# Window attention and a gated FFN on one core: the mask of 26 heads moves from VectorE into the score bank on TensorE

## The chip, the cores and the metric

The kernel runs on one core of a Trainium2 chip. The core has a matrix engine (TensorE, PE in the profile), VectorE (DVE), ScalarE (ACT), GpSimd (POOL), a queue engine that starts transfers (SyncE, SP), an on-chip memory (SBUF) and eight accumulation banks (PSUM) into which PE writes. The metric is the device time of one execution in microseconds (us). The kernel before takes 924.29 us, the median of 3 runs that lie between 923.28 and 925.11.

## What is computed

There are two stages. The first is attention with 8 batches, 8 heads, 512 local and 32 global rows and head dimension 64, all in float32. A local row sees the 32 global rows and the local rows at most 32 positions away. The second is an FFN over all 4352 rows, 512 to 2048 to 512 wide, with the gate `h * erf(softplus(h))`.

```
s_g = scale * q_g @ k_all.T;  out_g = softmax(s_g) @ v_all          # 32 global rows see all 544
s_ll = where(|i - j| <= 32, scale * q_l @ k_l.T, -1e9)
s_lg = scale * q_l @ k_g.T
out_l = softmax(concat(s_lg, s_ll)) @ concat(v_g, v_l)
x = concat(out_g, out_l)   as [8 * 544, 512]
h = x @ w_in;  out = (h * erf(softplus(h))) @ w_out
```

## The kernel before

**Attention.** Two heads share one load of queries and keys (`qk`, or `q` and `k` apart) and are scored together: 64 matmuls of 32 query rows against a window of 128 keys fill two PSUM banks `s`, one for each head, with 4 tiles of 128 by 128. For every head `mask_max` (VectorE) then adds a constant mask from SBUF (`mask`, part of the constants `cs`), writes the masked scores `sm` to SBUF and keeps the row extreme in `mx`, one instruction of its own for each of the 4 tiles. For the first 20 heads (`NBIAS`) ScalarE takes the exponentials in 4 instructions with `mx` as their bias; from head 20 on VectorE or GpSimd subtracts `mx` first, and ScalarE takes one exponential over all 512 columns. For the first 28 heads (`TURN`) PE transposes the probabilities back into the score bank `s`, VectorE or ScalarE copies them to `pt`, and 16 more matmuls with the values `va` and `vb` give the output in `s` again; for later heads VectorE transposes in blocks and two transfers through HBM (`tp`, `px`, `pt`) do the rest, with the output in a bank `o`. Every four heads the 32 global rows are done in banks `ga` and `gb`; `GTURN` says for how many of these groups PE makes the transposes.

**FFN.** To keep float32 accuracy every operand is split into a high and a low part (`xh`, `xl`, `winh`, `winl`, `wouth`, `woutl`, `gh`, `gl`), and every product is three matmuls of 512 columns. A batch is one chunk of 512 rows: 8 units `h` of 12 matmuls each, gates of 4 units on ScalarE (with a change of its function table ahead of softplus, of erf and of the next exponential), and 4 row tiles `op` of 24 matmuls. Pass 0 handles one half of the hidden width and pass 1 the other; only 4 of the 8 row blocks of the weights fit at a time. The weights arrive as 64-bit floats (`raw_in`, `raw_out`) and are turned into float32 (`top_in`, `top_out`) by `bits` on VectorE: a multiplication by a power of two, a shift, and two joint bit operations; 16 such pieces are turned during the first 150 us, 16 more near the end of pass 0.

**The order.** The kernel is written as a list of operations with their engines, a key and a guessed duration. `Program.schedule` plays them through on a model of the engines, takes the operation with the smallest key that is ready, chooses between the engines that an operation allows, and so fixes the order of every engine's instructions before the kernel is compiled. On the chip each engine runs its own list strictly in that order and waits where an operand is missing. While the model's PE has nothing to do before the time `FILL`, it puts in matmuls on a constant (`spare`) that keep the clock of PE up. These are real instructions: they take their time whether the data is there or not. So the numbers at the head of the file (keys, leads, `BIAS`, `HARM`, `SLACK`, ...) are priorities; a change of them moves instructions on all engines.

All work of a kind is issued through a helper, so that the profile shows L339 for every matmul, L340 for transposes on PE, L341 for ScalarE, L342 for its table changes, L343 for transfers and L351 for VectorE and GpSimd. The tile names tell them apart.

## Time and profile before

| what | us |
|---|---|
| median of 3 runs | 924.29 |
| the profiled execution's own time | 923.82 |
| its span in the profile | 921.9 |
| PE busy | 901.1 |
| VectorE busy | 639.3 |
| ScalarE busy | 514.3 |
| GpSimd busy | 400.9 |

The profiled execution is one of the kind that was timed: its time is 1.9 us more than its span, the part ahead of the first and behind the last recorded instruction. In the profile "busy" is the time in which at least one instruction of an engine runs. On PE the instructions overlap: a matmul of 512 columns has a duration of 0.39 us, but the next one starts 0.23 us later, so the cost of one in a row is the distance between starts. The same holds on VectorE, to a lesser degree.

### The profile page before, as it was taken

The page shows a single profiled execution, that of the slowest core. Times are in us where ns is not written, and L with a number is a line of the kernel's source. Part 1 is how long each engine was busy: PE and PEld are TensorE (multiplying, and loading weights), DVE is VectorE, ACT ScalarE, POOL GpSimd, SP SyncE. Part 2 cuts the span into 40 slices and gives each one's busy share as a digit, 9 for nine tenths or more (in the row PEclk, how much of TensorE's full clock was granted, in tenths as well). Part 3 has the DMA queues.
Part 4 walks back from the last instruction along what each step waited for, and adds up shares of the span by engine and source line. Part 5 has one row for each costly group of instructions (what it writes and reads, how often), then busy time and mean ns, then how long its engine had stood idle before and what let it go on. Part 6 is the DMA issues. An engine that isn't in the chain of part 4 may idle for free.

```text
span 921.9 us, 23134 instructions
## 1 busy us (share of the span) xinstructions
PE 901.1 (98%) x9363; PEld 751.5 (82%) x9363; DVE 639.3 (69%) x1616; ACT 514.3 (56%) x891; POOL 400.9 (43%) x318
## 2 busy tenths in 40 slices
PE   9889899999999999999999999999999999999998
PEld 7667667777777777878888888899898989999896
DVE  3799998565646766575589897868558575848533
ACT  4557956275645656455576655644646444546461
POOL 0212474164414343243366677735535455534320
PEclk9989999999999999999999999999999999999999
DMA  9788867597886887775462410222222250512203
GB/s 366 256 286 294 252 211 240 183 303 225 291 240 197 303 258 267 253 218 171 143 178 69 161 47 0 46 69 47 77 61 92 46 137 2 137 39 77 69 23 114
DMA packets 89322, 148.66 MB, mean 161 GB/s; under 512 B 11520, under 2 KB 52480, under 8 KB 89216
## 3 DMA queue, kind: packets, MB, share of 16 engines
q1 hardware_dynamic: 89024, 146.93, 50.9%
q8 instruction: 73, 1.20, 0.5%
q10 hardware_dynamic: 192, 0.26, 0.1%
q14 instruction: 33, 0.27, 0.1%
HBM read 108.89 MB, written 38.27 MB: 160 GB/s over the span
## 4 chain that ended last, share of the span: by engine, by line
PE 82%; DVE 12%; POOL 3%; issue 2%; ACT 1%; DMA 0%; DVEq 0%; POOLq 0%; ACTq 0%
PE op L339 37%; PE h L339 33%; PE s L339 4%; DVE top_out L351 3%; PE o L339 2%; PE spare L339 2%; DVE top_in L351 2%; PE ga L339 2%; DVE sm L351 1%; PE go L339 1%; DVE xh L351 1%; DVE xl L351 1%; PE s L340 1%; POOL xl L351 1%; DVE woutl L351 0%
## 5 line engine op out<-in xcount | busy, mean ns | idle before, releaser
L339 PE MATMUL op<-wouth,gh 128*128 128x512 f32 x544 | 217.3, 399 | 0.0
L339 PE MATMUL op<-woutl,gh 128*128 128x512 f32 x544 | 212.9, 391 | 0.0
L339 PE MATMUL op<-wouth,gl 128*128 128x512 f32 x544 | 212.5, 391 | 0.0
L351 POOL TENSOR_TENSOR sp<-sp,hs 128x512 f32<-128x512 f32 x94 | 135.0, 1453 | 165.1 <-ACT sp L341 120.1
L339 PE MATMUL h<-xh,winh 128*128 128x512 f32 (+1 forms) x464 | 165.2, 356 | 0.0
L339 PE MATMUL h<-xl,winh 128*128 128x512 f32 (+1 forms) x464 | 162.2, 350 | 0.2 <-POOL xl L351 0.2
L339 PE MATMUL h<-xh,winl 128*128 128x512 f32 (+1 forms) x464 | 162.2, 349 | 0.0
L351 POOL TENSOR_TENSOR gl<-sp,gh 128x512 fp32r<-128x512 f32 x78 | 111.9, 1442 | 103.9 <-ACT gh L341 72.8
L351 DVE TENSOR_TENSOR hs<-h,hs 128x256 f32<-128x256 f32 x196 | 76.4, 420 | 69.3 <-PE h L339 62.7
L339 PEld LDWEIGHTS op<-wouth,gh 128*128 128x128 f32 x544 | 102.5, 188 | 23.3 <-issue 2.0
L339 PEld LDWEIGHTS op<-wouth,gl 128*128 128x128 f32 x544 | 102.4, 188 | 22.3
L341 ACT ACTIVATE gh<-sp 128x512 fp32r<-128x512 f32 x113 | 69.2, 628 | 90.8 <-PE op L339 27.9
L339 PEld LDWEIGHTS op<-woutl,gh 128*128 128x128 f32 x544 | 102.6, 189 | 18.4
L342 ACT ACT_TABLE_LOAD x90 | 115.5, 1283 | 2.3 <-PEq L1281 0.7
L339 PEld LDWEIGHTS h<-xh,winh 128*128 128x128 f32 x464 | 87.8, 189 | 14.6 <-issue 1.0
L339 PEld LDWEIGHTS h<-xl,winh 128*128 128x128 f32 x464 | 87.9, 189 | 12.5 <-POOL xl L351 0.6
L339 PEld LDWEIGHTS h<-xh,winl 128*128 128x128 f32 x464 | 87.7, 189 | 11.6
L341 ACT ACTIVATE hs<-h 128x512 f32<-128x512 f32 (+1 forms) x66 | 36.5, 553 | 99.0 <-PE h L339 99.0
L341 ACT ACTIVATE sp<-hs 128x512 f32<-128x512 f32 x136 | 76.0, 622 | 16.1 <-DVE hs L351 15.7
L341 ACT ACTIVATE sp<-sp 128x512 f32<-128x512 f32 x136 | 74.8, 620 | 0.4
L351 POOL TENSOR_TENSOR sm<-sm,mx 128x512 f32<-128x512 f32 x26 | 28.7, 1112 | 101.3 <-DVE mx L351 93.7
L351 DVE CUSTOM_DVE_ANT_0 sm<-s,cs 128x128 f32<-128x128 f32 x256 | 57.1, 283 | 22.5 <-PE s L339 20.3
(176 smaller groups left out, 1603.6 us busy)
## 6 DMA issues: line engine op xcount, KB each, us to landing
vb<-in_vB_dram SPq DMA_DIRECT2D x32, 650.0 KB, 6.7
qk<-in_qk_dram SPq DMA_DIRECT2D x30, 656.0 KB, 6.7
rx<-xsc SPq DMA_DIRECT2D x52, 256.0 KB, 5.2
va<-in_vA_dram SPq DMA_DIRECT2D x32, 390.0 KB, 5.2
px<-tp SPq DMA_DIRECT2D x72, 128.0 KB, 4.3
pt<-px SPq DMA_DIRECT2D x18, 512.0 KB, 5.2
raw_in<-in_w_in_dram SPq DMA_DIRECT2D x16, 512.0 KB, 3.9
xsc<-xT SPq DMA_DIRECT2D x32, 256.0 KB, 4.5
```

Of the source, the lines that this page charges most:

```text
L339: pe = lambda n, *a, **k: pinned(nc.tensor.matmul(n, *a, **k))
L340: tr = lambda *a, **k: pinned(nc.tensor.transpose(*a, **k))
L341: act = lambda *a, **k: pinned(nc.scalar.activation(*a, **k))
L342: table = lambda name: pinned(nc.scalar.preload_act_table_set(name))
L351: return lambda *a, **k: pinned(f(*a, **k))
```

## The change

Five things change in the code.

1. For the first 26 heads (`PREMASK`) the mask no longer passes through VectorE's `mask_max`. At the start VectorE makes a bf16 copy of the mask (0 or -2^33) and of a unit matrix (`M16`, once). Ahead of the scores of a pair of heads PE writes the mask into each of the two banks by one bf16 matmul of 512 columns, and the 64 score matmuls add to it. VectorE takes the row maximum of each head by one plain reduction over the bank and multiplies the 4 maxima by -scale. ScalarE takes the exponentials from the bank, in 4 instructions with that bias, so heads 20 to 25 lose the subtraction and gain 3 ScalarE instructions; heads from 26 on subtract as before (`NBIAS` no longer decides).
2. The first step of `bits` (the multiplication by `REBASE`) becomes an operation of its own that ScalarE or VectorE may do.
3. PE transposes probabilities for 26 heads in place of 28, and for 7 groups of global rows in place of 8.
4. `FIRST` goes from 8 to 10: two more heads borrow FFN buffers for their attention tiles.
5. The priorities are new; several of them are now given by pass or by batch.

```diff
-SINCE, COLD, FILL, TICK, HEAT = 0.75, 3.5, 47.058, 3.41, 3200
+SINCE, COLD, FILL, TICK, HEAT = 0.75, 3.5, 52.16, 3.41, 3200
-HKEYS = ((0, -7.476), (4, -4.154), (22, 1.289), (64, 44.267))
+HKEYS = ((0, -7.916), (4, -4.313), (22, 2.061), (64, 45.265))
...
-FIRST = 8
+FIRST = 10
...
-NBIAS = 20
+NBIAS, PREMASK = 19, 26
...
-TURN, GTURN = 28, 8
+TURN, GTURN = 26, 7
...
+    M16 = Buf(mp, [P, 512], F32, "mask16", "os", 2)
...
+    def shorten():
+        m, i = halves()
+        dve.tensor_scalar(m, cs[:, :512], -1.0, -(2.0**33), op0=ALU.is_lt, op1=ALU.mult)
+        dve.tensor_copy(i, ident)
...
+                for n in range(2 if early else 0):
+                    m16, i16 = halves()
+                    pe(SS[n].ap.rearrange("p t k -> p (t k)"), i16, m16, start=True, stop=False)
...
-                                start=True,
-                                stop=True,
+                                start=not early,
+                                stop=not early or t == 3,
...
-        add({"DVE": 0.9}, key, mask_max, [S, CS], [SM, MX])
-        def exps():
+        def exps(src, k):
             for t in range(4):
-                act(SM.ap[:, t, :], SM.ap[:, t, :], AF.Exp, bias=MX.ap[:, t : t + 1], scale=-1.0)
+                act(SM.ap[:, t, :], src[:, t, :], AF.Exp, bias=MX.ap[:, t : t + 1], scale=k)
+        def plain_max():
+            dve.tensor_reduce(MX.ap, S.ap, axis=AX.X, op=ALU.max)
+            dve.tensor_scalar(MX.ap, MX.ap, -scale, None, op0=ALU.mult)
+        if early:
+            add({"DVE": 0.75}, key, plain_max, [S], [MX])
+            add({"ACT": 1.28}, key, lambda: exps(S.ap, scale), [S, MX, TAB], [SM])
+        else:
+            add({"DVE": 0.9}, key, mask_max, [S, CS], [SM, MX])
...
-            dve.tensor_scalar(TOP.ap.bitcast(F32), word(1).bitcast(F32), REBASE, None, op0=ALU.mult)
...
-        add({"DVE": 2.14}, key, bits, [RAW], [TOP])
+        add({"ACT": 0.62, "DVE": 0.42}, key, rebase, [RAW], [TOP])
+        add({"DVE": 1.72}, key, bits, [RAW], [TOP])
```

Three places show how the lists of the engines change. A name such as `s_6_0_2767` is the score bank 0 of the pair that begins with head 6; the last number only counts buffers, and the batch isn't printed. The first place is PE's list at its start, the scores of the first two heads. Before:

```order
L339 LDWEIGHTS const-bfloat16-1.0
L339 MATMUL spare<-const-bfloat16-1.0 128x256
L339 MATMUL s_0_0_188<-qk_0_124 32x128 x4
L339 MATMUL s_0_1_189<-qk_0_124 32x128 x4
...
L339 LDWEIGHTS const-bfloat16-1.0
L339 MATMUL spare<-const-bfloat16-1.0 128x256
```

Now:

```order
L339 LDWEIGHTS const-bfloat16-1.0
L339 MATMUL spare<-const-bfloat16-1.0 128x256
L339 LDWEIGHTS mask_194
L339 MATMUL s_0_0_213<-mask_194 128x512
L339 LDWEIGHTS mask_194
L339 MATMUL s_0_1_214<-mask_194 128x512
L339 MATMUL s_0_0_213<-qk_0_126 32x128 x4
L339 MATMUL s_0_1_214<-qk_0_126 32x128 x4
```

Two mask matmuls stand ahead of the scores. Before, 43 fillers (`spare`) stood ahead of these scores and 171 in all; now 61 stand ahead of them, and 176 in all.

The second place is VectorE's list around the maximum of head 6 of batch 1. Before:

```order
L351 COPY gxT_0_1388<-gb_0_1075 128x64
L351 STREAM_TRANSPOSE xT_3_1390<-xn_2_1241 128x512
L351 TENSOR_SCALAR top_in_3_1_1396<-raw_in_3_1_1085 128x512
L351 TENSOR_SCALAR top_in_3_1_1396<-top_in_3_1_1396 128x512
L351 SCALAR_TENSOR_TENSOR top_in_3_1_1396<-raw_in_3_1_1085,top_in_3_1_1396 128x512 x2
L351 ISA sm_6_1424,mx_6_1425<-s_6_0_1352,cs 128x128
L351 ISA mx_6_1425 128x1
```

Now:

```order
L351 COPY gxT_0_1445<-gb_0_1093 128x64
L351 TENSOR_REDUCE mx_6_1447<-s_6_0_1354 128x4
L351 TENSOR_SCALAR mx_6_1447<-mx_6_1447 128x4
L351 TENSOR_REDUCE mx_7_1452<-s_6_1_1355 128x4
L351 TENSOR_SCALAR mx_7_1452<-mx_7_1452 128x4
L351 TENSOR_SCALAR top_in_2_1_1450<-top_in_2_1_1450 128x512
L351 SCALAR_TENSOR_TENSOR top_in_2_1_1450<-raw_in_2_1_1260,top_in_2_1_1450 128x512 x2
```

The pair of rows `ISA sm` and `ISA mx`, which came four times for a head, has become one reduction and one small product, and the row `top_in<-raw_in` of this piece of the weights is gone from VectorE's list (it is in ScalarE's). Of the 16 pieces of the first 150 us, 10 lose this row.

The third place is PE's list ahead of the first output product of the FFN (`op_0_0`), in batch 3 of the attention. Before:

```order
L339 MATMUL s_4_0_2790<-qk_2_2654 32x128 x4
L339 MATMUL s_4_1_2791<-qk_2_2654 32x128 x4
...
L339 MATMUL ga_0_2621<-va_0_2197,gt_0_2744 32x65 x2
L339 MATMUL ga_0_2621<-va_1_2486,gt_0_2744 32x65 x2
...
L339 MATMUL op_0_0_2863<-wouth_0_1579,gh_0_0_1875 128x512
L339 MATMUL op_0_0_2863<-woutl_0_1580,gh_0_0_1875 128x512
```

Now:

```order
L339 MATMUL s_6_0_2767<-qk_3_2583 32x128 x4
L339 MATMUL s_6_1_2768<-qk_3_2583 32x128 x4
...
L339 MATMUL h_1_5_2845<-xh_1_0_2187,winh_2_688 128x512
L339 MATMUL h_1_5_2845<-xl_1_0_2192,winh_2_688 128x512
...
L339 MATMUL gb_0_2552<-cs,xg_0_2866 128x64
L339 MATMUL op_0_0_2875<-wouth_0_1579,gh_0_0_1835 128x512
L339 MATMUL op_0_0_2875<-woutl_0_1580,gh_0_0_1835 128x512
```

Now the scores of one more pair (heads 6 and 7), the 12 products of one more unit (`h_1_5`) and one product of the global rows (`gb`) stand ahead of `op_0_0`; the value products of heads 2 and 3 of batch 3, which stood ahead of it, come after it.

More of the change, by code (lines that the diff above doesn't have):

```diff
@@ L58 @@
 SEVEN = (0, 1, 2, 3, 4, 5, 6)
-SUMS = 82.024
-TURN, GTURN = 28, 8
+SUMS = (82.024, 82.124)
+TURN, GTURN = 26, 7
 SET_EXP = "exp_and_others"
@@ L375, with halves @@
     half = cs[:, 512 + P + 64 :]
-    load(HKEYS[0][1] - QLEAD + 0.001, CS, cst, 360)
+    load(HKEYS[0][1] - QLEAD[0] + 0.001, CS, cst, 360)
     PG = fixed(attn.tile([P, NENT // 4, P], F32, name="pg"))
+    M16 = Buf(mp, [P, 512], F32, "mask16", "os", 2)
+    def halves():
+        t = M16.ap.bitcast(BF16)
+        return t[:, :512], t[:, 512 : 512 + P]
+    def shorten():
+        m, i = halves()
+        dve.tensor_scalar(m, cs[:, :512], -1.0, -(2.0**33), op0=ALU.is_lt, op1=ALU.mult)
+        dve.tensor_copy(i, ident)
+    if PREMASK:
+        add({"DVE": 0.6}, HKEYS[0][1], shorten, [CS], [M16])
     add({"POOL": 0.7}, -99, lambda: pool.memset(PG.ap, 0.0), writes=[PG])
@@ L424, in attention @@
                 QKB = abuf([P, QK], f"qk_{pn}", "qk", 2)
-                load(key - QLEAD, QKB, qk[b, p], 671)
+                load(key - QLEAD[b > 1], QKB, qk[b, p], 671)
                 st["qk"] = ([QKB], lambda: QKB.ap[:, :SQ], lambda: QKB.ap[:, SQ:])
@@ L430, in attention @@
             VB = abuf([P, 2 * (NWIN - 6), D + 1], f"vb_{pn}", "vb", 2)
-            load(key - VLEAD, VA, vA[b, p], 400)
-            load(key - VLEAD, VB, vB[b, p], 666)
+            load(key - VLEAD[b > 1], VA, vA[b, p], 400)
+            load(key - VLEAD[b > 1], VB, vB[b, p], 666)
             st["va", p % 2], st["vb"] = VA, VB
@@ L457, in attention @@
         MX = abuf([P, 4], f"mx_{nm}", "mx", 2)
-        biased = b * H + h < NBIAS
+        early, biased = (b * H + h) // 2 * 2 < PREMASK, b * H + h < NBIAS
         def mask_max():
@@ L472, in mask_max @@
                 )
-        add({"DVE": 0.9}, key, mask_max, [S, CS], [SM, MX])
-        def exps():
+        def exps(src, k):
             for t in range(4):
-                act(SM.ap[:, t, :], SM.ap[:, t, :], AF.Exp, bias=MX.ap[:, t : t + 1], scale=-1.0)
-        if biased:
-            add({"ACT": 1.28}, key, exps, [MX, TAB], [SM])
+                act(SM.ap[:, t, :], src[:, t, :], AF.Exp, bias=MX.ap[:, t : t + 1], scale=k)
+        def plain_max():
+            dve.tensor_reduce(MX.ap, S.ap, axis=AX.X, op=ALU.max)
+            dve.tensor_scalar(MX.ap, MX.ap, -scale, None, op0=ALU.mult)
+        if early:
+            add({"DVE": 0.75}, key, plain_max, [S], [MX])
+            add({"ACT": 1.28}, key, lambda: exps(S.ap, scale), [S, MX, TAB], [SM])
+        else:
+            add({"DVE": 0.9}, key, mask_max, [S, CS], [SM, MX])
+        if early:
+            pass
+        elif biased:
+            add({"ACT": 1.28}, key, lambda: exps(SM.ap, -1.0), [MX, TAB], [SM])
         else:
@@ L767, in word, with rebase @@
             return RAW.ap.bitcast(I32).rearrange("p (n two) -> p n two", two=2)[:, :, n]
+        def rebase(e):
+            if e == "ACT":
+                act(TOP.ap.bitcast(F32), word(1).bitcast(F32), AF.Copy, scale=REBASE)
+            else:
+                dve.tensor_scalar(TOP.ap.bitcast(F32), word(1).bitcast(F32), REBASE, None, op0=ALU.mult)
         def bits():
-            dve.tensor_scalar(TOP.ap.bitcast(F32), word(1).bitcast(F32), REBASE, None, op0=ALU.mult)
             dve.tensor_scalar(
@@ L1177, in load_late @@
         kind, src, u = ("in", w_in, i) if i < NU else ("out", w_out, i - NU)
-        load_unit(kind, src, 1, u, late[2 * i], late[2 * i + 1], WB0 + WBS * i, [ATTN])
+        load_unit(kind, src, 1, u, late[2 * i], late[2 * i + 1], LATE[i], [ATTN])
     late = [(wb_pool, f"b{i}") for i in range(11)] + [
@@ L1193 @@
                 for u in range(2):
-                    sums(u, SUMS + 0.1 * u)
+                    sums(u, SUMS[u])
             if ps == 1 and c in SEVEN:
-                X = seven_x(c, s - XLEAD)
+                X = seven_x(c, s - XLEAD[2])
                 G = {}
@@ L1205 @@
             span = c == SPAN
-            X = kept[0] if span and ps else load_x(ps, c, s - XLEAD)
+            X = kept[0] if span and ps else load_x(ps, c, s - XLEAD[ps])
             us = [unit(ps, c, v, X, s + v) for v in range(n)]
@@ L1210 @@
             for a, z in ((0, 2), (2, 3), (3, 4)) if last else [(i, i + 4) for i in range(0, n, 4)]:
-                G += gate(ps, c, us[a:z], s + z + GOFF, range(a, z))
-            OP = project(ps, c, G, s + 4 + POFF, range(NU), kept[1] if span and ps else None, not span or ps == 1)
+                G += gate(ps, c, us[a:z], s + z + GOFF[ps], range(a, z))
+            OP = project(ps, c, G, s + 4 + POFF[ps], range(NU), kept[1] if span and ps else None, not span or ps == 1)
             if span:
```

34 lines of the change are left out of this document (18 added, 16 removed).

## The prediction

> **What bounds the kernel now.** I read the page first, then the busy time by stage, then PE's waits in the stage that has any.
>
> ```profile
> span 921.9 us, 23134 instructions
> PE 901.1 (98%) x9363; PEld 751.5 (82%) x9363; DVE 639.3 (69%) x1616; ACT 514.3 (56%) x891; POOL 400.9 (43%) x318
> ```
>
> PE is busy for all but 20.8 us, so this is a PE kernel as a whole. The next view has, for each stretch, its length, then the busy time of PE, weight loads, VectorE, ScalarE and GpSimd, and PE's granted clock.
>
> ```profile
> 0.00:37.00 37.00, 33.63 (x694) 26.33 (x695) 18.10 (x96) 16.36 (x44) 3.60 (x7) 0.95 0.90 348
> 37.00:147.50 110.50, 100.25 (x2123) 77.94 (x2120) 107.24 (x380) 79.25 (x174) 39.06 (x30) 0.97 0.80 257
> 147.50:917.80 770.30, 767.25 (x6554) 647.26 (x6550) 513.32 (x1140) 418.72 (x675) 358.23 (x282) 1.00 0.46 139
> 917.80:921.90 4.10, 0.00 (x0) 0.00 (x0) 0.69 (x1) 0.00 (x0) 0.00 (x0) 1.00 0.51 128
> ```
>
> From 147.5 us to the last matmul PE idles for 3.05 us in 770. So the end is fixed by two things: when PE gets onto that steady track, and how much work is then left. Before it PE idles 13.6 us (3.37 and 10.25), and from 37 to 147.5 us VectorE is busy for 107.24 of 110.5 us. That stretch is VectorE's. PE's waits up to 150 us (total, times, longest) agree:
>
> ```profile
> PE ga L339 <- issue: 2.6, 1, 2.6
> PE s L340 <- ACT sm L341: 2.3, 2, 1.7
> PE ga L340 <- ACT pg L341: 1.6, 2, 1.4
> PE s L339 <- ACT pt L341: 1.4, 2, 1.1
> ...
> PE spare L339 <- PEq L1281: 0.8, 1, 0.8
> ```
>
> The first (at 24.6 us) waits for nothing that the profile shows, and the last is the start; neither is VectorE's. The rest are ScalarE or VectorE results that come at the end of VectorE's queue.
>
> **What PE gains and loses.** Prices are distances between starts, or pieces of the chain that ended last.
>
> ```profile
> 71.10 0.39 PE L339 MATMUL h<-xl,winh 128*128 128x512 f32 x1
> 71.33 0.40 PE L339 MATMUL h<-xh,winl 128*128 128x512 f32 x1
> ...
> 7.57 1.09 PE s L339 x64
> ...
> 12.35 0.44 PE s L340 x4
> ...
> 17.52 1.22 PE spare L339 x10
> ...
> 139.94 0.33 PE ga L340 x3
> 140.27 0.33 PE gb L340 x3
> ```
>
> No bf16 matmul of 512 columns is in the trace. The nearest rows are the split-float one of 512 columns, 0.23 us, and the bf16 filler of 256 columns, 0.122 us, which doubled is 0.24. I take 0.23: 26 of them, one for each head, are +6.0 us. Two heads fewer are transposed on PE, 2 x 0.44, and one group of global rows fewer, 0.66: -1.5. Fillers go from 171 to 176, 5 x 0.12: +0.6. PE's own work grows by 5.1 us, and nothing takes that off again after 147.5 us. The change is paid unless it closes holes before.
>
> **What VectorE gains.** The rows are one head's old maximum, a reduction, a dependent pair of small operations, and one independent small operation.
>
> ```profile
> 70.20 0.28 DVE L351 CUSTOM_DVE_ANT_0 sm<-s,cs 128x128 f32<-128x128 f32 x1
> ...
> 71.04 0.65 DVE L351 TENSOR_REDUCE gm<-ga 128x1 f32<-128x480 f32 x1
> 71.61 0.28 DVE L351 CUSTOM_DVE_ANT_0 sm<-s,cs 128x128 f32<-128x128 f32 x1
> ...
> 18.79 0.21 DVE L351 TENSOR_REDUCE gm<-gb 128x1 f32<-128x64 f32 x1
> 19.04 0.21 DVE L351 TENSOR_SCALAR gn<-gm 128x1 f32<-128x1 f32 x1
> 19.22 0.69 DVE L351 COPY pt<-s 128x512 f32<-128x512 f32 x1
> ```
>
> The old maximum runs from 70.20 to 71.04: 0.84 us a head. The new reduction over 512 elements is not in the trace; that over 480 holds the engine for 0.57 us (71.04 to 71.61), which makes 0.60, and the product with -scale behind it costs 0.07 if it needn't wait for the reduction's result and up to 0.26 if it must (0.68 for the reduction to finish, 0.18 until the next starts, as in 18.79 to 19.22). So 0.67 to 0.86 a head; I take 0.75, a product that waits but itself is short. That saves 0.09 x 26 = 2.3 us, with -4.4 and +0.5 as ends. So the mask itself relieves VectorE by little.
>
> [...]
>
> The other edits weigh more. These are the first step of one piece of the weights and the next one, and the group of subtractions:
>
> ```profile
> 67.98 0.39 DVE L351 TENSOR_SCALAR top_in<-raw_in 128x512 f32<-128x512 f32 x1
> 68.40 0.43 DVE L351 TENSOR_SCALAR top_in<-top_in 128x512 int32<-128x512 int32 x1
> ...
> L351 DVE TENSOR_TENSOR sm<-sm,mx 128x512 f32<-128x512 f32 x18 | 15.4, 858 | 0.2
> ...
> 142.21 1.42 DVE L351 SCALAR_TENSOR_TENSOR top_out<-raw_out,top_out 128x512 int32<-128x512 int32 x2
> ```
>
> I count both lists up to the last bit operation of the 16 early pieces, which ended at 143.6 us. Ten rescalings go to ScalarE, 10 x 0.42 = -4.2. Subtractions on VectorE fall from 4 to 1, 3 x 0.86 = -2.6. The bf16 mask costs +0.6. Against this the new order gives VectorE work that others did: 2 casts of weights, 3 copies `gt`, 2 `xT`, 1 `hs`, 1 `pt`, an `sp` and a `winl` more, a `gl` and a transpose fewer, together about +3.8 at 0.35 to 0.6 each. With the maxima it is 2.3 + 4.2 + 2.6 - 0.6 - 3.8 = 4.7 us less. The ends, 2 and 7, are those of the maxima.
>
> ScalarE takes ten rescalings and, for heads 20 to 25, four exponentials for one:
>
> ```profile
> L341 ACT ACTIVATE sm<-sm,mx 128x128 f32<-128x128 f32 x80 | 24.8, 390 | 13.4 <-DVE mx L351 13.4
> L341 ACT ACTIVATE sm<-sm 128x512 f32<-128x512 f32 x44 | 26.9, 630 | 30.6 <-POOL sm L351 21.5 <-DVE rs L351 4.8 <-DVE sm L351 3.9
> ```
>
> That is 10 x 0.63 + 6 x (4 x 0.39 - 0.63) = 11.9 us at most, on top of 79.25 in 110.5 us, and some copies leave it for VectorE. It stays under 83 %; I cost it at nothing, and a rival below takes that cover away.
>
> **The start.** PE issues its fillers whether the data is there or not.
>
> ```profile
> 0.77 6.79 PE spare L339 x43
> ...
> 31.27 1.43 PE s L339 x64
> ```
>
> The first scores come 18 fillers (2.1 us) and two mask matmuls (0.5) later. Up to the scores of the fourth pair (31.27 us) the lists have 117 fillers before and 119 now, and 8 mask matmuls: those scores move by 0.2 + 1.8 = 2.0 us. VectorE's saturated time starts with them, so I put the 2.0 us on VectorE's side. Transfers are issued in nearly the same order there; I cost their moves at nothing, since PE waited for no load.
>
> **The sum.** The mark is the first output product, `op_0_0`, where the steady track begins.
>
> ```profile
> 147.54 4.33 PE op L339 x18
> ```
>
> The new list has more ahead of it: 12 products (2.7), one pair's scores (1.1) and one product of the global rows (0.2), less the values of two heads (0.9): +3.1. The old kernel would be at this mark, so shifted, at 150.6. For the new one there are two bounds. PE: 147.5 - 13.6 idle + 3.1 + 6.0 masks - 0.9 transposes + 0.6 fillers = 142.7, and with the two holes that are not VectorE's (2.6 and 0.8) 146.1. VectorE: 143.6 - 4.7 + 2.0 = 140.9 for the weights, and the same 4.0 us from there to `op_0_0`: 144.9. PE is now the later one, by a little, so most of the 10.25 us of holes should close. Two engines with nearly equal sums in fixed orders still wait for each other at places; for that I take a fifth of the old holes, 2.0 us, because the fully VectorE-bound stretches in which PE was also supplied with FFN products had hardly a hole. That puts the mark at 148.1, 2.5 us ahead; the last global group's transposes after it (0.66) make 3.2. From 923.8 us, the execution profiled, this is **920.6 us**. The median, 924.3, is 0.5 us above that execution; I keep the figure. The ends of this sum are no hole left, 918.6, and 5 us of holes, 923.6.
>
> **Rivals.**
>
> *The masks are paid and the holes stay (slower).* The holes before 147.5 us may be the length of a path (scores, maximum, exponential, transpose, copy, values) and not VectorE's load; and a dependent product could cost the whole 0.26 us, so that a head costs VectorE 0.86 for 0.84. Then the path is no shorter, and each pair stands 0.46 us later behind its masks. All holes kept give 923.8 + 5.1 = 928.9 us; it turns slower where more than 5.1 of the 10.25 us stay. For it: the largest waits end with ScalarE. Against it: VectorE's 97 %.
>
> *All holes close and the clock holds (clearly faster).* PE's granted clock, the third column from the right, falls after two holes of 1.7 and 1.4 us (the longest of the second and third row of PE's waits):
>
> ```profile
> 55.00:60.00 5.00, 3.61 (x44) 2.84 (x43) 4.90 (x19) 2.80 (x9) 0.00 (x0) 0.58 1.00 410
> 60.00:65.00 5.00, 5.00 (x151) 4.09 (x150) 4.83 (x19) 1.55 (x4) 0.00 (x0) 0.73 0.69 194
> ```
>
> At 0.58 and 0.73 the work of these 10 us cost 0.42 x 3.61 + 0.27 x 5.00 = 2.9 us more than at full clock. The new list has 21 fillers for 16 and 7 more between the transposes there. If this stretch stays warm and no hole is left, the time is 918.6 - 2.9 = 915.7. [...]
>
> *ScalarE takes VectorE's place (no change).* Its busy time is the fourth of the five in a row:
>
> ```profile
> 85.00:90.00 5.00, 4.82 (x86) 3.25 (x84) 4.86 (x28) 4.97 (x8) 1.44 (x2) 1.00 0.94 350
> 90.00:95.00 5.00, 5.00 (x32) 3.99 (x29) 4.90 (x8) 4.97 (x13) 2.45 (x3) 1.00 0.96 323
> ```
>
> From 85 to 95 us it is full already (4.97 of 5). If it delays four or five exponentials by a rescaling of 0.63 each, 3 us of holes come back and the time is about 923.5, within 0.2 % of before. That the edits don't act as they say is no rival: the lists show them.
>
> **Chances.** Forecast, 919 to 922.4: 0.42. Clearly faster, 915 to 919: 0.18. No change that a measurement could tell (it tells about 0.2 %, 1.85 us: 922.4 to 926.1): 0.20. Slower, 926.1 to 929: 0.20. So faster 0.60, same 0.20, slower 0.20. The range takes the forecast, the other two cases and the nearer part of the slow one: 915.5 to 927.5. Cases that are faster hold most; the forecast's own range is 918.6 to 923.6.
>
> **What would show it.** Right: VectorE under 0.80 us a head, the last early weights near 141 us, `op_0_0` near 148, PE idle before it near 5.5 us, no new idle behind. Wrong: PE's idle before `op_0_0` still over 10 us; ScalarE named as releaser with ten rescalings ahead of exponentials; a reduction near 0.9 us; a stall like that at 24.6 us twice; or idle between 150 and 900 us because the late weights or chunks come late under the new keys.

## The result: slower by 0.6 %

The changed kernel takes 929.8 us (median of 5 runs, 928.9 to 931.1), 1.006 times the time of the kernel before, with a 95 % interval of 1.0035 to 1.0085. The kernel before had five runs by then, 921.5 to 926.9, with the median 924.29 as above. The forecast was 920.6, and the range ended at 927.5.

The page of the changed kernel, for its busy times and for the queue that carries instructions (packets, MB, share of the 16 engines):

```profile
span 929.0 us, 23011 instructions
...
PE 904.4 (97%) x9378; PEld 752.1 (81%) x9380; DVE 638.5 (69%) x1476; ACT 512.7 (55%) x895; POOL 376.1 (40%) x300
...
q8 instruction: 74, 1.21, 0.5%
```

PE is busy 3.3 us longer than before and idle 3.8 us longer (24.6 for 20.8): both halves of the 7.1 us by which the span grew. The profiled execution took 931.1 us, 1.3 more than the median. Taken apart, the 7.1 us between the two profiled executions are:

| part of PE's time | before, us | changed, us | difference |
|---|---|---|---|
| work: busy time less what the lowered clock cost in it | 894.78 | 898.24 | +3.46 |
| what the lowered clock cost | 6.35 | 6.15 | -0.20 |
| waits called "issue" (explained below) | 3.78 | 9.26 | +5.48 |
| other holes ahead of the first output product | 10.14 | 6.91 | -3.23 |
| other holes behind it, to the end | 6.86 | 8.45 | +1.59 |

The same stretches as before, in the same columns (length, then busy time of PE, weight loads, VectorE, ScalarE, GpSimd, and PE's granted clock):

```profile
0.00:37.00 37.00, 33.72 (x630) 26.14 (x636) 17.94 (x45) 13.74 (x39) 3.48 (x7) 0.95 0.89 339
37.00:147.50 110.50, 99.73 (x2033) 75.55 (x2025) 102.73 (x259) 77.15 (x184) 31.05 (x24) 0.98 0.75 251
147.50:917.80 770.30, 763.92 (x6691) 644.90 (x6691) 516.43 (x1172) 421.83 (x674) 341.57 (x269) 1.00 0.47 141
```

Up to 147.5 us PE idles 3.28 + 10.77 = 14.05 us, where 13.6 were to shrink to 5.4; behind it 6.4, where there were 3.05. So the holes were not closed, but they are other holes. PE's waits over the whole execution (total, times, longest):

```profile
PE s L339 <- issue: 5.5, 5, 3.2
PE gb L339 <- DVE xg L351: 2.6, 1, 2.6
PE h L339 <- DVE xh L351: 2.6, 1, 2.6
PE ga L339 <- issue: 2.4, 1, 2.4
PE s L339 <- DVE xn L351: 1.8, 1, 1.8
PE o L339 <- issue: 1.4, 1, 1.4
```

Waits for ScalarE, the largest of those with a named releaser before, are small now. The largest are called "issue": PE waits for nothing that the profile shows. They were 3.8 us before (2.6 at 24.6 us, 0.9 and 0.3 later) and are 9.3 now. And `op_0_0`, the mark of the prediction, starts later than the place where the forecast put the old list at the same work (150.6) and not earlier:

```profile
L339 PE MATMUL op<-wouth,gh x544: 389/389/504, 153.4 to 924.0; 128*128 128x512 f32 x182
```

VectorE's part of it, by two groups between 37 and 160 us (count, busy time, mean ns of one) and then three single products with GpSimd's work beside them (start, duration):

```profile
L351 DVE TENSOR_REDUCE mx<-s 128x4 f32<-128x512 f32 x19 | 12.9, 679 | 0.4 <-PE s L339 0.4
...
L351 DVE TENSOR_SCALAR mx<-mx 128x4 f32<-128x4 f32 x19 | 6.4, 337 | 0.7
```

```profile
47.50 0.17 DVE L351 TENSOR_SCALAR mx<-mx 128x4 f32<-128x4 f32 x1
...
95.41 2.51 POOL L351 TENSOR_TENSOR gl<-sp,gh 128x512 fp32r<-128x512 f32 x2 [0.61 <-ACT gh L341]
...
97.09 0.87 DVE L351 TENSOR_SCALAR mx<-mx 128x4 f32<-128x4 f32 x1
...
117.98 2.54 POOL L351 TENSOR_TENSOR sp<-sp,hs 128x512 f32<-128x512 f32 x2
118.07 1.22 DVE L351 TENSOR_SCALAR mx<-mx 128x4 f32<-128x4 f32 x1
```

The product of four numbers a row takes 0.17 us alone. Beside GpSimd it ends when GpSimd's operation ends: at 97.96, where the pair of GpSimd operations ends at 97.92, and at 119.29, where the first of a pair of 1.27 us ends at 119.25. With it a head holds VectorE for 0.95 us in the mean (26 heads, from the start of the reduction to the next operation or the product's end; 0.82 in the 19 heads where the product isn't stretched), against 0.85 before. The edit that was to relieve VectorE by 2.3 us loads it with 2.6 more.

All 7 products that were stretched (of 26) ended within 0.05 us of the end of a GpSimd operation. What held them no trace shows.

### The profile page after: what moved, and what is told of

Read it like the earlier page. It is cut to its first block, busy times and chain, and to the rows that moved or that the text cites. A ratio compares the mean times of both kernels' runs of the same rounds, so it can differ in the third digit from the quotient of the medians.

```text
span 929.0 us, 23011 instructions
## 1 busy us (share of the span) xinstructions
PE 904.4 (97%) x9378; PEld 752.1 (81%) x9380; DVE 638.5 (69%) x1476; ACT 512.7 (55%) x895; POOL 376.1 (40%) x300
## 4 chain that ended last, share of the span: by engine, by line
PE 91%; DVE 6%; issue 2%; ACT 1%; POOL 1%; DMA 0%; SPq 0%; DVEq 0%; POOLq 0%
PE op L339 40%; PE h L339 37%; PE s L339 5%; PE spare L339 2%; PE o L339 2%; PE ga L339 2%; DVE top_out L351 1%; PE s L340 1%; PE go L339 1%; DVE mx L351 1%; DMA vb<-in_vB_dram 0%; DVE xl L351 0%; PE gb L339 0%; DVE top_in L351 0%; POOL sx L351 0%
## 5 line engine op out<-in xcount | busy, mean ns | idle before, releaser
L351 POOL TENSOR_TENSOR sp<-sp,hs 128x512 f32<-128x512 f32 x92 | 129.9, 1431 | 158.3 <-ACT sp L341 151.0
L351 POOL TENSOR_TENSOR gl<-sp,gh 128x512 fp32r<-128x512 f32 x74 | 102.9, 1395 | 148.8 <-ACT gh L341 119.2
L339 PEld LDWEIGHTS h<-xl,winh 128*128 128x128 f32 x464 | 88.2, 190 | 11.8
L339 PEld LDWEIGHTS h<-xh,winl 128*128 128x128 f32 x464 | 88.1, 190 | 11.9
L351 DVE TENSOR_TENSOR gl<-sp,gh 128x512 fp32r<-128x512 f32 x62 | 59.1, 965 | 19.3 <-ACT gh L341 18.7
L351 POOL TENSOR_TENSOR xl<-rx,xh 128x256 fp32r<-128x256 f32 (+1 forms) x50 | 51.7, 1060 | 47.2 <-ACT xh L341 40.6
```

The source lines that it names most:

```text
L339: pe = lambda n, *a, **k: pinned(nc.tensor.matmul(n, *a, **k))
L351: return lambda *a, **k: pinned(f(*a, **k))
```

## The experiments

Four theories.

- **A**: PE pays for the 26 mask matmuls, and nothing gives that back.
- **B**: VectorE sets the stretch up to `op_0_0`, and the product behind the maximum burdens it.
- **C**: PE's code comes late. The queue above moves 74 pieces of 16.4 KB, and PE's trace has some 18,900 instructions, 255 for each piece. Where PE uses up a piece before the next is there, it waits, and the profile calls that wait "issue"; "code wait" below is this theory's name for it.
- **D**: the new priorities cost the time, not the mask.

"Place" below is the place of the pieces' ends in the program. A filler split into two halves makes two more PE instructions at the start, and two merged ones make two fewer, for nearly the same PE time (43 fillers took 6.8 us in the kernel before and 6.4 us with 32 of them split in 16; 61 took 8.5 and 8.3 us in two executions of the changed kernel and 8.7 us with 60 of them merged in 13); everything behind then lies elsewhere in the pieces, in the same order.

| kernel | median us | ratio to before (95 %) | issue waits in its trace, us |
|---|---|---|---|
| before | 924.29 | 1 | 3.8 |
| changed | 929.80 | 1.006 (1.0035 to 1.0085) | 9.3 |
| 1 changed, no mask matmuls | 934.52 | 1.0122 (1.0084 to 1.016) | 19.8 |
| 2 changed, product on ScalarE | 930.83 | 1.0069 (1.0042 to 1.0097) | 9.7 |
| 3 new priorities, old maximum | 947.44 | 1.0249 (1.0224 to 1.0273) | 6.7 |
| 4 old priorities, new maximum | 942.0 | 1.0191 (1.0162 to 1.022) | 8.8 |
| 5 changed, place +64 | 927.15 | 1.0012 (0.9991 to 1.0034) | 1.6 |
| 6 changed, place -60 | 932.29 | 1.0071 (1.0045 to 1.0097) | 8.9 |
| 7 before, place +64 | 920.49 | 0.995 (0.9928 to 0.9971) | 7.2 |
| 8 before, place -80 | 931.23 | 1.0063 (1.0041 to 1.0085) | 11.8 |
| 9 as 1, place +80 | 929.59 | 1.0039 (1.0018 to 1.0059) | 11.8 |
| 10 as 2, place +64 | 922.81 | 0.9961 (0.994 to 0.9982) | 4.4 |
| 11 as 5, no row maximum | 924.57 | 0.998 (0.9957 to 1.0003) | 7.0 |
| 12 as 7, masks on PE beside the old maximum | 921.33 | 0.9953 (0.9935 to 0.9971) | 0 |
| 13 as 2, place -60 | 927.27 | 1.0029 (1.0001 to 1.0057) | 6.8 |
| 14 changed again | 930.71 | 1.0071 (1.0048 to 1.0094) | 8.2 |
| 15 as 5, masked maximum on VectorE | 937.99 | 1.0148 (1.0108 to 1.0188) | 10.3 |
| 16 as 7, one more product a head | 928.6 | 1.0056 (1.0026 to 1.0085) | 5.1 |

The kernel before had medians of 924.6 to 926.9 beside these. The waits are those of one execution and the times medians of several, so the two columns don't follow each other to the microsecond. They also come from runs that were taken together with other runs of the kernel before, so between kernels of different groups the ratios compare better than the medians.

### 1. Without the mask matmuls

```diff
-                for n in range(2 if early else 0):
-                    m16, i16 = halves()
-                    pe(SS[n].ap.rearrange("p t k -> p (t k)"), i16, m16, start=True, stop=False)
...
-                                start=not early,
-                                stop=not early or t == 3,
+                                start=True,
+                                stop=True,
```

> The changed kernel, same order on every engine, without the 26 mask matmuls (and their 26 weight loads) ahead of the scores; the scores start their banks themselves. The mask is left out of the result. Theory A (PE pays for the masks): a pair's masks and scores held PE for 1.47 us where the scores alone took 1.09, so 13 pairs give back 4.9 us: 929.8 becomes 924.9. Theory B (the stretch up to op_0_0 is set by VectorE, whose row maximum now costs 0.98 us a head): PE only waits where it issued masks, and the time falls by less than 1.5 us, to 928.3 or more. Theory C (PE's code comes late in dense stretches: the waits called issue were 9.3 us in the changed kernel, 3.8 before): besides the 4.9 us some issue waits go too, and the time is under 923.

It took 934.5, more than with the masks. No theory asked for that, but its waits say where it came from:

```profile
PE s L339 <- issue: 10.9, 5, 3.7
PE h L339 <- issue: 4.7, 2, 2.4
PE ga L339 <- issue: 3.5, 2, 3.1
```

What these waits have in common is their number in PE's program. The first instruction behind each wait of 0.15 us or more, counted over all PE instructions in the trace:

```
before:       961, 5569, 9921                                         each 193 behind a multiple of 256
changed:      959, 1983, 2751, 4031, 4287, 6335, 11455                each 191 behind one
no masks:     705, 961, 2753, 4033, 4289, 5057, 5569, 6593, 11457     each 193 behind one; and 3412
```

The 3.2 us of the changed kernel stand at its instruction 4287, in the middle of a pair's scores, and the 3.7 us here at 4289, at another place of the work. The waits belong to the count of instructions, not to an operation. That without the masks 256 instructions are worked through sooner, so that more ends of pieces find PE waiting, is the likely reason for the longer waits here; 52 instructions fewer also move the ends, and this run doesn't tell the two apart.

### 2. The product on ScalarE

```diff
         def exps(src, k):
+            if early:
+                act(MX.ap, MX.ap, AF.Copy, scale=-scale)
...
-            dve.tensor_scalar(MX.ap, MX.ap, -scale, None, op0=ALU.mult)
```

> The changed kernel, but the product of the row maximum with -scale (128x4, SBUF to SBUF) runs on ScalarE ahead of the four exponentials instead of on VectorE behind the maximum; the planner's numbers are the same. That product took VectorE 0.17 us alone and 0.49 to 1.22 us beside GpSimd, 0.27 us start to start in the mean, 26 times 0.27 = 7.0 us. Theory B (VectorE sets the stretch before op_0_0): up to 19 of them lie on its path, 5 us, and the time falls from 929.8 to about 925. Theory A (PE's own work and holes of other kinds set it): the two PE holes that ended with VectorE's xn and xg (1.85 and 2.61 us) shrink at most, and the time is 928 to 930; ScalarE's added 0.2 us a head may take that back.

930.8: no gain, as A asked, while 9.7 us of code waits stayed. Experiments 10 and 13 repeat it at other places, with another answer.

### 3 and 4. Half of the change each, planned anew

```diff
-NBIAS, PREMASK = 19, 26
+NBIAS, PREMASK = 19, 0
```

> The new priorities and the free choice of engine for the rescaling, but every head with the old maximum (four masked reductions on VectorE, no mask matmul, no bf16 mask); the order is planned anew under the new numbers. If the mask edit is what costs (A or B): 929.8 less the 4.9 us of masks, less some of 26 x 0.14 = 3.6 us of VectorE, so 921 to 925. If the new priorities cost the time (theory D): 928 or more.

For the other half the old table of constants stands with `PREMASK = 26`, and `rebase` runs on VectorE inside `bits`.

> The old priorities and constants, rescaling on VectorE as before, but masks on PE and the plain maximum for the first 26 heads; the order is planned anew under the old numbers. If the mask edit is what costs (A or B): 924.3 + 4.9 = 929 or more, and the new priorities then saved something if it is above 930. If the new priorities cost the time (theory D): 923 to 926.

Both are slower than either kernel, 947.4 and 942.0. In 3 the planner's new list makes PE wait for ScalarE in the late attention:

```profile
PE o L339 <- ACT pg L341: 9.9, 2, 5.8
```

In 4 it waits for VectorE's `xg` instead, 6.9 us. The priorities fit the operations they were set with, and half of a change under the other half's table is a third list. So these two divide nothing between mask and order, and every later experiment keeps the list and changes only what an entry issues. One thing they do tell. PE's two holes at the start of the second pass over the FFN are these in kernel 4, and the same (1.2 to 1.3 and 0.3 us) in the kernel before and in every kernel made from its list:

```profile
604.54 0.38 PE L339 MATMUL h<-x,winh 128*128 128x256 f32 x1 [1.23 <-ACT x L341]
605.27 0.39 PE L339 MATMUL h<-x,winh 128*128 128x256 f32 x1 [0.34 <-DVE x L351]
```

In the changed kernel they are these, and 2.6 to 2.8 and 0.7 to 0.9 us in every kernel made from its list:

```profile
593.98 0.38 PE L339 MATMUL h<-xh,s1h 128*128 128x256 f32 x1 [2.59 <-DVE xh L351]
595.25 0.58 PE L339 MATMUL h<-xl,s1h 128*128 128x256 f32 x1 [0.89 <-DVE xl L351]
```

That is 2.59 + 0.89 - 1.23 - 0.34 = 1.9 us more, and it goes with the new list, not with the mask: kernel 4 has the new maximum and the old holes. (Kernel 3, planned anew, has neither pair.)

### 5 to 8. The same work at other places of the pieces

```diff
-    prog.filler(0.11, lambda: pe(spare, warm[:, :P], warm, start=True, stop=True), 256, SINCE, FILL)
+    told = []
+
+    def idle():
+        told.append(0)
+        if len(told) <= 32:
+            for z in range(0, 256, P):
+                pe(spare[:, z : z + P], warm[:, :P], warm[:, z : z + P], start=True, stop=True)
+        else:
+            pe(spare, warm[:, :P], warm, start=True, stop=True)
+
+    prog.filler(0.11, idle, 256, SINCE, FILL)
```

For fewer instructions every second one of the first 60 or 80 fillers is left out and the one ahead of it has 512 columns.

> The changed kernel with the first 32 fillers split into two matmuls of 128 columns each: 64 more instructions on PE (32 matmuls, 32 weight loads) before anything else, no other work and no other order. Every wait called issue in the traces so far stands at the same instruction number modulo 256 of PE (191 in the changed kernel, 193 before), whatever operation stands there. Theory C (PE's code comes in pieces of 256 instructions, and a piece that is used up before the next has come makes PE wait): the ends of the pieces move back by 64 instructions in the program; if a piece needs 5.5 us, the trace's own times of 256 instructions give 7.7 us of waits instead of 10.7, so 3 us less, 927. Theory A (masks) and B (VectorE): nothing changes by this, 929 to 931.

> The changed kernel with the first 60 fillers merged in pairs into 30 matmuls of 512 columns: 60 PE instructions fewer, the same PE time, the same order. Theory C: the ends of the code pieces fall later in the program, in the middle of the dense runs; by the same estimate 14.4 to 17 us of waits instead of 10.7, so 933 to 936. Theories A and B: 929 to 931.

> The kernel before with 64 more PE instructions at the start (32 fillers split into two matmuls of 128 columns). Theory C: by the trace of before 9.6 us of waits in place of 12.8 if a piece needs 5.5 us; only 3.8 were measured, so 1 to 3 us less, 921 to 923. Theories A and B: 924.3, no change.

> The kernel before with its first 80 fillers merged in pairs into 40 matmuls of 512 columns: 80 PE instructions fewer by 22 us, the same PE time. Theory C: by the trace of before 18.5 us of waits in place of 12.8 if a piece needs 5.5 us, so 5 us more, 928 to 931, as slow as the changed kernel. Theories A and B: 924.3.

The four times lie at or within a microsecond of what theory C said: 927.2 for 927, 932.3 for 933 to 936, 920.5 for 921 to 923, 931.2 for 928 to 931. For kernel 6 this proves little: its ratio, 1.0071, is that of the changed kernel when it ran again (14), and its waits are no longer. In kernel 5 the waits in scores shrank to the first row, and in kernel 8 one of 5.4 us came up at 150 us, where the kernel before had 0.9 us at the same count:

```profile
PE s L339 <- issue: 1.4, 2, 1.0
```

```profile
PE ga L339 <- issue: 5.4, 1, 5.4
PE o L339 <- issue: 3.0, 2, 2.4
PE s L340 <- issue: 2.6, 1, 2.6
```

So the place counts: 124 instructions move the changed kernel by 5 us, 144 the old one by 11, with no change in their work. In kernels 5 and 8 the waits in the trace moved with the time, as C asks. In kernel 7 they did not: its trace has 7.2 us of issue waits where the kernel before has 3.8, at the same span (922.0 for 921.9). That execution took 923.9 us, 3.4 over its median, so it may not be typical; how kernel 7 gained is not shown. Whether the place is the whole of the difference the medians can't tell either. The mean of the three places is 929.7 us for the changed kernel and 925.3 for the old one, but with places that differ by up to 11 us among themselves three of each are too few to make 4.4 us of that certain.

The column "issue" also misses some. At instruction 703, which is 191 behind a multiple of 256, PE stood still in kernels 5, 10 and 12, for 1.4, 1.0 and 2.0 us; the profile puts these waits down to ScalarE's `pg`, though what follows is a transpose of `sm`. In kernels 5 and 12 that `sm` was ready over 1.5 us earlier, so these were code waits under another name. In kernel 12:

```profile
PE s L340 <- ACT pg L341: 2.0, 1, 2.0
```

Kernel 7 is also the fastest of all, faster than both kernels: 0.995 of before, with nothing but 32 fillers cut in half.

### 9. Without the mask matmuls, at another place

The edits of 1 and 5, with 40 fillers split.

> The changed kernel without its mask matmuls (the mask is left out of the result) and with 80 more PE instructions at the start (40 fillers split in two), which moves the ends of the code pieces out of its dense runs: by the trace of the kernel without masks 5.1 us of code waits are left of 9.0 if a piece needs 4.5 us, 12.6 of 17.6 if it needs 5.5. Theory A (PE pays for the masks): the changed kernel with its own 64 instructions took 927.2, less 4.9 us of masks: 922 to 923. Theory B (the stretch is set by VectorE): no faster than 926. Against the kernel without masks as it stood (934.5) Theory C alone asks for 929 to 930.

929.6: what C alone asked for, and A not. Some 6 us of PE's work less than in kernel 5 gave nothing back: 11.8 us of issue waits stand in its trace, 1.6 in that of kernel 5 (3.0 with the one at 703).

### 10 and 13. The product on ScalarE, at two other places

The edits of 2 and 5, and of 2 and 6.

> The changed kernel with 64 more PE instructions at the start and the product with -scale on ScalarE, to be set beside the same without the second edit (927.2). Theory B: VectorE gets 5 us off its path up to op_0_0, so 923 to 925. Theory A: 926 to 928, since PE's waits for VectorE's xn and xg are the only ones that can shrink.

> The changed kernel with 60 PE instructions fewer at the start (932.3 by itself) and the product with -scale on ScalarE. Theory B (the product behind the maximum costs the path): 4 us less, as with 64 instructions more, 927 to 929. Theory C (the ends of the code pieces decide, and what VectorE gives back PE then waits for code): 931 to 933, as without them.

922.8 against 927.2, and 927.3 against 932.3: 4.3 and 5.0 us less (4.7 and 3.9 by the ratios). B holds at these places. At the kernel's own place (2) it does not. In kernel 10 the mark stands where the forecast had it (148.1), and its time is inside the forecast's own range of 918.6 to 923.6:

```profile
L339 PE MATMUL op<-wouth,gh x544: 389/389/504, 147.6 to 914.7; 128*128 128x512 f32 x182
```

So with the product off VectorE and the code at another place the list reached the forecast's mark and time, though not by its sum: 10.7 us of holes stand ahead of the mark in place of 5.4, and PE is busy for 136.9 us up to it in place of 142.7, with no time lost to a lowered clock there.

### 11. No row maximum

```diff
-            dve.tensor_reduce(MX.ap, S.ap, axis=AX.X, op=ALU.max)
-            dve.tensor_scalar(MX.ap, MX.ap, -scale, None, op0=ALU.mult)
+            pass
...
-                act(SM.ap[:, t, :], src[:, t, :], AF.Exp, bias=MX.ap[:, t : t + 1], scale=k)
+                if early:
+                    act(SM.ap[:, t, :], src[:, t, :], AF.Exp, scale=k)
+                else:
+                    act(SM.ap[:, t, :], src[:, t, :], AF.Exp, bias=MX.ap[:, t : t + 1], scale=k)
```

> The changed kernel with 64 more PE instructions at the start and no row maximum at all for the first 26 heads: VectorE is given back the whole 0.98 us a head, 19 of them before op_0_0, 18 us of its 103 in 110 us. The maximum and its subtraction are left out; the exponentials are taken of the scores as they are. Theory B: with VectorE so far relieved the holes before op_0_0 that are not code go, 7 to 11 us, and the time is 918 to 920. Theory A: VectorE does not set the end; the chain of scores, exponentials, transposes, values does, and PE's own sum: 924 to 927, at most 3 us better than 927.2.

924.6, so 2.6 us less than kernel 5, for some 18 us less on VectorE ahead of `op_0_0`. B asked for 918 to 920; in the strong form, that VectorE alone sets the stretch, it falls. The first two stretches of this kernel, in the columns used above:

```profile
0.00:37.00 37.00, 34.33 (x735) 27.48 (x738) 12.39 (x32) 12.99 (x45) 3.48 (x7) 1.00 0.91 347
37.00:147.50 110.50, 102.45 (x2155) 79.16 (x2152) 93.79 (x247) 75.50 (x189) 36.83 (x28) 1.00 0.82 265
```

VectorE is busy for 93.79 us of 110.5 now, and PE still idles 2.67 + 8.05 = 10.7 us up to 147.5. 7.0 us of that are code waits, which were 1.6 in kernel 5 (3.0 with the one at 703), while the waits with another releaser ahead of the mark fell from 10.0 to 2.7. Relief of VectorE closes its holes, and a part of the gain goes into code waits.

### 12. The masks' PE time in the old kernel

```diff
             def scores():
+                for n in range(2 if b * H + h < 26 else 0):
+                    pe(SS[n].ap.rearrange("p t k -> p (t k)"), warm[:, :P], warm, start=True, stop=True)
```

> The kernel before with 64 more PE instructions at the start (920.5 by itself) and with two matmuls of 512 columns ahead of each of the first 13 pairs of scores, whose result the scores overwrite: PE pays for masks and VectorE keeps its old maximum. Theory A: PE's 4.9 us are paid in full, 925 to 926. Theory B: a good part lies in the holes in which PE waits for VectorE and ScalarE, 921 to 923. Theory C: on top of either, the 52 instructions move the ends of the pieces again, by up to 3 us either way.

921.3 for 920.5. PE's work (its busy time less what the lowered clock cost in it) is 899.7 us for 893.9, so the 26 matmuls do cost 0.22 us each; yet only 0.8 us of these 5.8 came out at the end. That does not settle A, because 52 more instructions move the ends of the pieces too. In the two traces the issue waits fell from 7.2 us to none (2.0 with the one at 703) and the cost of the lowered clock from 5.5 to 1.7 us, while the waits with another releaser ahead of the mark hardly changed, 7.4 us for 8.0. So in these two executions the masks' time was made up by the place and not by VectorE's holes. What masks cost at a fixed place no run shows.

### 14. The changed kernel again

> The changed kernel as it is, beside the others. All theories: 929 to 931; Theory C: its waits called issue stand at the same instruction numbers (959, 1983, 2751, 4031, 4287, 6335, 11455) as in its first trace, with other lengths.

930.7, and the waits stand at the same seven instructions. The one at 4287 has 3.19 us for 3.18, the one at 6335 0.83 for 1.40.

### 15. The old maximum in the new list

```diff
-            dve.tensor_reduce(MX.ap, S.ap, axis=AX.X, op=ALU.max)
-            dve.tensor_scalar(MX.ap, MX.ap, -scale, None, op0=ALU.mult)
+            for t in range(4):
+                dve.tensor_tensor_reduce(
+                    S.ap[:, t, :], S.ap[:, t, :], mask[:, t, :], -scale, 3.0e38,
+                    op0=ALU.add, op1=ALU.min, accum_out=MX.ap[:, t : t + 1],
+                )
...
-            add({"ACT": 1.28}, key, lambda: exps(S.ap, scale), [S, MX, TAB], [SM])
+            add({"ACT": 1.28}, key, lambda: exps(S.ap, -1.0), [S, MX, TAB], [SM])
```

> The changed kernel with 64 more PE instructions at the start, its order kept on every engine, but the mask edit undone for the first 26 heads: no mask matmuls, and four masked reductions in place of the plain maximum and its product (they write the masked scores back over the scores, where the exponentials read them). A head costs VectorE 0.84 us for 0.98, PE 4.9 us less in all. If the mask edit is what costs: 927.2 less 3 to 5 us, 922 to 924. If it is the new order: 926 to 928. Theory C: the 52 instructions fewer move the ends of the pieces, which cost the changed kernel without masks all that it gained, so 929 to 930.

938.0, and not a clean undoing. The four reductions that write back into the score bank hold VectorE for 1.40 us a head (mean over the 26 heads), where those that write to SBUF held it for 0.85. So it loads VectorE with 0.45 us a head more than the new maximum, 11.7 us over 26 heads, and the time is 10.8 us longer. That is no proof that the load was paid: without the masks the ends of the pieces lie elsewhere, and set beside kernel 5's its trace has 10.3 us of issue waits for 1.6 and loses 11.1 us to the lowered clock for 1.6. It decides nothing on the mask, and little on VectorE's load.

### 16. Only the product, in the old kernel

```diff
                     accum_out=MX.ap[:, t : t + 1],
                 )
+            if b * H + h < 26:
+                dve.tensor_scalar(MX.ap, MX.ap, 1.0, None, op0=ALU.mult)
```

> The kernel before with 64 more PE instructions at the start (920.5 by itself), and on VectorE one more small product (128x4, SBUF to SBUF, by 1.0) behind each of the first 26 maxima; PE's code is the same, so the ends of its pieces are. Theory B: 26 products of 0.27 us, some 19 of them before op_0_0, on an engine that is busy 97 % there: 3 to 5 us more, 923.5 to 925.5. Theory A and C: at most 1 us more.

928.6 for 920.5, more than B asked. PE's matmuls and weight loads and their order are the same, so this is the cleanest of the experiments. The group, between 37 and 160 us:

```profile
L351 DVE TENSOR_SCALAR mx<-mx 128x4 f32<-128x4 f32 x19 | 7.7, 408 | 0.7
```

Those 19 have a mean of 0.41 us, all 26 one of 0.34, and from the start of a product to the next operation they hold VectorE for 0.26 us, 6.7 us in all. 8.1 us come out at the end (9.8 by the ratios). In the trace it is PE's waits with another releaser ahead of the mark that grew, from 8.0 to 11.9 us, and not the issue waits (5.1 for 7.2). So load added to VectorE is paid in full here (16), while load taken away is paid back by a part (10, 11, 13) or not at all (2).

## Why the prediction was wrong, point by point

**What bounds the kernel.** Half right. VectorE's load matters (16), but the first row of PE's waits was passed over: "The first (at 24.6 us) waits for nothing that the profile shows". It was the end of a code piece. Such waits were carried through the sum as the 2.6 us of that one. The kernel's own file has a term for them: with `BLOCK, FETCH = 256, 2.908` the planner (`stalls`, `runs`) lets PE enter 256 new instructions no sooner than 2.9 us after it entered the last 256. Where PE stood at such an end the traces show 3.4 to 8.4 us (below), so the plan has room for waits that it doesn't see. Whether a larger `FETCH` would plan around them was not tried.

**The step that failed: "most of the 10.25 us of holes should close".** 2.0 us of holes were to be left ahead of the mark, and 3.4 that are not VectorE's. 14.05 are there up to 147.5 us. Those with a releaser in the trace did shrink, from 9.3 to 6.0 us, but code waits ahead of the mark grew from 3.5 to 7.1. Kernel 11 shows that no price of the maximum alone would have saved the step: without any maximum 10.7 us are left, 7.0 of them for code. The two bounds, PE's sum and VectorE's, were not the only ones. The prediction's own sign of being wrong, "a stall like that at 24.6 us twice", came true: seven code waits, two of them over 2 us.

**The term that was mis-sized: a head on VectorE.** "I take 0.75, a product that waits but itself is short." The reduction was as forecast (0.68 us, 0.72 to the next start). The product is short by itself, 0.17, but waits for GpSimd in 7 of 26 heads: 0.31 in the mean (0.34 over the 19 heads of the group above), and 0.95 for a head. That is +2.6 us over 26 heads in place of -2.3, outside the range of 0.67 to 0.86, since the nearest row was a product of another shape, taken where GpSimd was idle.

**VectorE's sum.** 4.7 us less up to the last early piece of the weights was the forecast. Counted in the two traces, from each operation's start to its end or the next start, VectorE was held 122.0 us up to there before and 119.1 now: 2.9 less, so the other terms gave some 3 us more than forecast and made up for part of the heads. But VectorE stood still 5.2 us longer, 26.8 for 21.6 with its start counted; 2.7 us of that are a wait for PE's transposes at 137 to 140 us, behind the hole of 2.6 us in which PE waits for VectorE's `xg` at 132 us. So each engine also waited for the other. The weights end at 145.9 us and not at 140.9:

```profile
144.48 1.42 DVE L351 SCALAR_TENSOR_TENSOR top_out<-raw_out,top_out 128x512 int32<-128x512 int32 x2
```

**PE's price.** 0.23 us a mask was right (0.22 in 12). PE's work grew by 3.5 us in the two traces, where 5.1 were forecast. That it is "paid unless it closes holes" was the right condition: holes closed, but code waits opened in their place.

**ScalarE at nothing.** Right. The waits that end with ScalarE before 147.5 us fell from 5.3 us to 1.0.

**The start.** 2.0 us later was forecast for the fourth pair's scores; 1.3 came (the masks and scores begin at 32.6 us).

**The mark.** 148.1 forecast, 153.4 measured, 5.3 us late. In PE's sum, the holes ahead of it are 14.0 us for 5.4, and PE is busy for 139.3 us for 142.7. (The forecast carried along the 4.7 us that the lowered clock had cost the old kernel up to there; it cost 3.2 now.) The weights were 5.0 us late too, but from their end to the mark it took 7.5 us in place of 4.0, so they don't explain the mark. Two code waits of the changed kernel that the old one did not have:

```profile
114.67 0.66 PE L339 MATMUL s<-qk 64*32 64x128 f32 x27 [3.18 <-issue]
...
181.65 0.22 PE L339 MATMUL o<-va,pt 128*32 128x65 f32 x1 [1.40 <-issue]
```

**No new idle behind the mark.** Wrong by 3.3 us (6.38 for 3.05): 1.9 at the second pass, which goes with the new list (D holds for this part, by 3 and 4), and 1.4 + 0.7 of code waits at 181.65 and 367.28 us, less 0.7 of old waits that are gone.

**The rivals.** The slower one (928.9) had the time almost right: the holes stayed in sum, and a head did cost more than before, by 0.10 us where it allowed for 0.02. That the time came so close is in part luck: it had the old holes stay on an unchanged path, and the trace shows the old holes shrunk and code waits in their place. The rival on the clock was right in kind: the loss it spoke of is gone, 1.00 for 0.58 and 0.73. But the clock now falls behind a hole of 2.6 us at 132 us (the third column from the right):

```profile
55.00:60.00 5.00, 4.01 (x138) 3.17 (x130) 4.96 (x13) 4.06 (x12) 1.72 (x2) 1.00 0.80 282
60.00:65.00 5.00, 5.00 (x117) 3.62 (x114) 4.86 (x13) 1.70 (x4) 0.00 (x0) 1.00 1.00 387
130.00:135.00 5.00, 2.69 (x74) 1.91 (x78) 4.36 (x15) 1.70 (x7) 1.26 (x1) 0.86 0.75 250
135.00:140.00 5.00, 5.00 (x33) 3.98 (x25) 1.70 (x5) 2.53 (x8) 0.00 (x0) 0.80 0.97 306
```

**What stays open.** At the place +64 the product (4.3 us, 10) and the second pass (1.9) add up to 6.2 of the 6.7 us between kernels 5 and 7. That leaves next to nothing for PE's 5.3 us more work there, and single effects need not add, so it is a sum and no proof. At the kernel's own place, where the change was measured, taking the product away gave nothing (2). That PE there waits for code in place of VectorE is likely, since 9.7 us of code waits stay, but how the 5.5 us divide between product, code and the masks' work at that place is not shown. Nor is the price of the masked maximum in the new list, since 15 was no clean undoing, or that of the masks alone (1, 9 and 12 move the code). What is shown is that a move of 64 instructions brings the changed kernel to 1.0012 of before (0.9991 to 1.0034).

## What to carry to other kernels

Price a small operation on VectorE by where it will run, not by its size: beside GpSimd a product of four numbers a row took up to 1.22 us, 0.17 us alone, on the engine that had no time to spare (busy for 102.73 of 110.5 us). A wait that "waits for nothing" can be a wait for code: count the instructions ahead of it. Here 90 of 97 such waits stood at nearly the same count modulo 256, 191 to 193, and that pointed at the code. An experiment that adds or removes PE instructions moves PE's code as well (124 instructions and 5 us between kernels 5 and 6); those here that left PE's matmuls alone (2, 10, 11, 13, 16) read more plainly than those that did not (1, 9, 12, 15). And before a change of 0.5 % is believed, in either direction, move the code by some dozens of instructions without changing the work: here that alone was worth -0.5 % and +0.6 % to the kernel before.

## What the runs showed of the hardware

**PE's code came in pieces of 256 instructions, one ahead.** In all 18 traces 90 of the 97 issue waits of 0.15 us or more, 132 of their 141 us, stand 191 to 193 instructions behind a multiple of 256 of PE's count. At the 83 ends of pieces before 200 us at which PE issued nothing for over 0.4 us, the transfer of the piece began 3.4 us after the end of the piece before (0.6 to 5.5), took 1.1 us (0.9 to 1.8), and PE went on 1.4 us after it (1.2 at the least): 6.0 us in the mean from one end to the next (3.4 to 8.4). A pair's masks and scores, 132 instructions, take 1.5 us, so a run of such work outpaces its code. Issue waits lasted up to 5.4 us at one end, and 1.6 to 19.8 us together in the traces that have any.

**A long wait can be paid twice, and need not be.** In the changed kernel the granted clock is 0.86 and 0.80 in the ten microseconds around and behind the hole of 2.6 us at 132 us (rows above), 0.14 x 2.69 + 0.20 x 5.00 = 1.4 us more. The longer wait of 3.18 us at 111 to 115 us lowered nothing:

```profile
110.00:115.00 5.00, 1.82 (x73) 1.03 (x67) 4.86 (x12) 4.96 (x11) 2.63 (x2) 1.00 0.93 354
115.00:120.00 5.00, 5.00 (x57) 3.68 (x43) 4.69 (x9) 2.85 (x10) 5.00 (x5) 1.00 0.47 122
```

Kernel 1, with five waits of 2 us or more for its code, had a mean granted clock of 0.985 over its span, and kernel 5, with none, 0.997.

The fillers, which are there to keep the clock up, stand in every kernel, so no run shows what they alone do for it. With them PE has no idle time from 7.6 to 24.5 us of the kernel before, at a granted clock of 1.00.

**A small product beside GpSimd.** 0.17 us alone, 0.30 to 1.22 in 7 of 26 heads beside it, each time to the end of GpSimd's operation; reductions and copies that read the score banks (`mx`, `pt`) kept their 0.66 to 0.69 us there.
